# Twelve weight splits, each made one or two slots sooner, in a linear attention and rational feed-forward kernel

## Chip, cores and metric

The kernel runs on one core of one Trainium2 chip. The metric is the device time of one execution in microseconds (us); lower is better. A time stands as the median of several runs. One further execution was recorded by the hardware profiler, and all durations of single instructions come from that one.

## What is computed

Linear attention over 8 batches, 8 heads, 576 positions and 64 channels, with a normalisation of each head's output, and behind it a feed-forward layer whose activation is a quotient of two polynomials:

```python
kv  = einsum('bhsd,bhse->bhde', k, v)
out = einsum('bhsd,bhde->bhse', q, kv)
x   = out / sqrt(mean(out * out, axis=-1) + 1e-6) * g_norm   # then heads side by side: 4608 x 512
h   = x @ w_in                                               # 512 -> 2048
P   = a[0] + a[1] * h + a[2] * h**2 + a[3] * h**3
Q   = 1 + abs(b[0]) * abs(h) + abs(b[1]) * h**2
y   = (P / (Q + 1e-6)) @ w_out                               # 2048 -> 512
```

All inputs are float32. The kernel receives `w_in` and `w_out` as the 64-bit words that the host handed over (`I64` in the code) and makes float32 of them itself.

## The kernel before, in words

**Tiles and slots.** The 4608 tokens are cut into 9 tiles `t` of 512. In each tile the 2048 hidden channels are cut into 16 blocks `c` of 128. One pair (t, c) is a slot; the main loop (L657) runs over slots `i` = 16 t + c, 144 in all. In slot `i` the following is issued, engine by engine, in the order of the code (the scheduler is off, L605, so that each engine executes its instructions in just this order):

- ScalarE (ACT) and VectorE (DVE) turn the block `h` of slot `i` into the activation: `ew_a` (L472) begins with ACT's L477 on `h`, DVE's L479 makes `q`; `ew_d` (L506) splits the activation of slot `i - 1` into a rounded part `gh` (ACT, L513) and a rest `gl` (DVE, L514); `ew_b` and `ew_c` (L485, L493) finish with DVE's L503.
- TensorE (PE) does `gemm2` of slot `i - 2` (L517: 4 groups that add to `acc`), matmuls of the attention of the next tile, and `gemm1` of slot `i + 1` (L459: the `h` that ACT reads next). So PE works one to two slots ahead of and behind the elementwise engines. `h` has two buffers.

**Split weights.** In the first tile PE multiplies unsplit float32 operands (L463 for blocks below 8, L526). From the second tile on each product is done as three matmuls in a faster format: rest times high, high times low, high times high (L467 to L469 for `gemm1`, L530 to L532 for `gemm2`). For this each of the 16 weight units, ("wi", c) or ("wo", c), each holding two blocks, has to be split once into a high part and a low part. That takes three steps:

1. `split_w` (L219): ACT rounds the unit, 128 x 1024, into the high part (L231) at the end of the slot's `ew_b` work. It also notes the rest of the work in the list `lows`.
2. `low_by_transfer` (L236) in the *next* slot: POOL writes the negated high part into the low part's place (L237). A manual dependency holds this back until DVE has made `q` of that slot (L661).
3. POOL then issues a transfer of 512 KB which adds the float32 weight to that place (L238), so that weight minus high part is left. PE's L531 or L468 waits for this transfer to land.

The planner is a table written out by hand, `schedule` (L124): for each unit the slot of its fetch, of its conversion from 64-bit words, and, third, of its split; then the names of the memory cells of its raw words, of its float32 form and of its split form. The split form goes to cells that older units have left. A unit ("wi", c) is first used by `gemm1` of slot 16 + c, which PE does in slot 15 + c; a unit ("wo", c) by `gemm2` of slot 16 + c, which PE does in slot 18 + c. `at_slot(2, i)` (L674) picks the units to be split in slot `i`.

**What else lies around.** In the slots up to 15 the tile 0 work also contains the conversion of the last weights (ACT L195 and L188, DVE L207 and L215), the attention of tile 1 with its broadcast reads of the normalisation through DRAM (`att_rd`, `att_rb`, L409 to L423, on SP's queue), its use (`att_norm`, DVE L427) and the split of tile 1's `x` (ACT L290, DVE L294). In the second tile, slots 16 to 31, the attention of tile 2 takes slots 16 to 29, among them the reciprocal root (ACT L276 to L278) in slot 25, `att_norm` in slots 27 to 29 and the split of the new `x` in slot 30.

Of the kernel before, what the change touches and what calls it, by code (L numbers as in the profile page):

```python
# [23 lines left out]
def linear_attention_then_rational_ffn(  # L24
# [93 lines left out]
    def f32(t):  # L118
# [3 lines left out]


    schedule = {  # L124
# [16 lines left out]
    }  # L141
    units = list(schedule)

# [604 lines left out]
```

## Time and profile before

| | |
|---|---|
| median of 3 runs | 897.2 us (896.45 to 897.43) |
| the profiled execution's own time | 896.94 us |
| its span, first to last instruction | 895.2 us |
| granted clock of PE, mean | 0.997 of full |
| PE busy | 882.9 us, 99% |
| DVE busy | 768.4 us, 86% |
| ACT busy | 694.4 us, 78% |
| POOL busy | 77.9 us, 9% |

Times within the execution are in us from the start of the span. In a row of the timeline stand start, length, engine, line, operation, output<-inputs, and in brackets, if the engine sat idle before it, for how long and what ended that. A row of the waits gives who waited for whom, us in total, how often, and the longest. Matmuls overlap: their length is not what one costs; the distance between the starts of two neighbours is. A busy PE in the first table is therefore no proof that it waits for nothing.

### The profile page before, as it was taken

The numbers are of one execution on the slowest core, as the hardware profiler recorded it, in microseconds if no ns is written. First come the engines' busy times: TensorE is split into PE (matmuls) and PEld (weight loads), VectorE is DVE, ScalarE is ACT, GpSimd is POOL, SyncE is SP. The second block draws the span as 40 slices with busy tenths as digits, with TensorE's granted clock in tenths as the row PEclk, the third lists the DMA queues.
The fourth block names the chain that finished last, engine by engine and source line by source line (L and its number), as shares of the span: only waits on it lengthen the run. The fifth ranks groups of instructions, "written<-read, shape, count | busy, mean of one in ns | idle before, by whom it ended". The sixth has DMA issues, their size and how long they took to land.

```text
span 895.2 us, 11762 instructions
## 1 busy us (share of the span) xinstructions
PE 882.9 (99%) x4326; PEld 686.5 (77%) x4326; DVE 768.4 (86%) x1214; ACT 694.4 (78%) x1173; POOL 77.9 (9%) x85
## 2 busy tenths in 40 slices
PE   8999999998999999999999999999999999999998
PEld 5445567777787888878887888788878887888886
DVE  3888898878988898889978997899788988898887
ACT  5899979786887788777877787768767887777665
POOL 2053326413100000000000000000000000000000
PEclk9999999999999999999999999999999999999999
DMA  9997328534321203220320132012202020201001
GB/s 368 352 301 210 77 56 209 133 59 96 94 101 41 48 12 119 83 49 1 130 73 21 38 118 83 13 48 71 71 12 49 1 71 12 49 1 48 0 1 48
DMA packets 26810, 75.35 MB, mean 84 GB/s; under 512 B 2624, under 2 KB 2624, under 8 KB 26752
## 3 DMA queue, kind: packets, MB, share of 16 engines
q1 hardware_dynamic: 23328, 64.10, 20.8%
q0 software_dynamic: 2848, 9.44, 5.8%
q10 hardware_dynamic: 576, 1.05, 0.3%
q8 instruction: 34, 0.56, 0.3%
q14 instruction: 24, 0.20, 0.1%
HBM read 55.58 MB, written 9.57 MB: 73 GB/s over the span
## 4 chain that ended last, share of the span: by engine, by line
PE 78%; DVE 8%; ACT 7%; DMA 4%; issue 1%; POOL 1%; SPq 0%; DVEq 0%; POOLq 0%; ACTq 0%
PE h L467 12%; PE acc L531 12%; PE acc L532 12%; PE acc L530 12%; PE h L469 12%; PE h L468 12%; DMA wohl<-wow 2%; DVE q L479 2%; PE kvp L324 1%; DMA first<-in_first_dram 1%; DVE u L497 1%; PE ms L392 1%; DMA wol<-wow 1%; PE op L375 1%; PE op L376 1%
## 5 line engine op out<-in xcount | busy, mean ns | idle before, releaser
L477 ACT ACTIVATE d<-h 128x512 f32<-128x512 f32 x143 | 85.7, 599 | 154.9 <-PE h L469 152.1
L479 DVE SCALAR_TENSOR_TENSOR q<-d,b1abs,q 128x512 f32<-128x512 f32 x143 | 107.2, 750 | 96.6 <-ACT q L478 95.8
L467 PE MATMUL h<-x,wihl 128*128 128x512 f32 (+1 forms) x420 | 167.7, 399 | 0.0
L469 PE MATMUL h<-x,wihl 128*128 128x512 f32 (+1 forms) x420 | 162.8, 388 | 0.0
L468 PE MATMUL h<-x,wihl 128*128 128x512 f32 (+1 forms) x420 | 162.8, 388 | 0.0
L531 PE MATMUL acc<-wol,gh 128*128 128x512 f32 x316 | 123.7, 392 | 2.6 <-DMA wol<-wow 2.6
L530 PE MATMUL acc<-woh,gl 128*128 128x512 f32 x316 | 123.5, 391 | 0.8 <-DVE gl L514 0.8
L532 PE MATMUL acc<-woh,gh 128*128 128x512 f32 x316 | 123.4, 391 | 0.0
L490 ACT ACTIVATE d<-q,bias 128x512 f32<-128x512 f32 x143 | 105.7, 739 | 12.5 <-DVE q L479 11.1
L480 ACT ACTIVATE u<-h,na 128x512 f32<-128x512 f32 x143 | 112.6, 788 | 0.0
L491 ACT ACTIVATE d<-d,bias 128x512 f32<-128x512 f32 x143 | 103.6, 724 | 4.7
L497 DVE SCALAR_TENSOR_TENSOR u<-u,na,d 128x512 f32<-128x512 f32 x143 | 106.7, 746 | 0.0
L487 DVE SCALAR_TENSOR_TENSOR u<-u,na,h 128x512 f32<-128x512 f32 x143 | 106.1, 742 | 0.6
L495 DVE SCALAR_TENSOR_TENSOR q<-q,d 128x512 f32<-128x512 f32 x143 | 98.6, 690 | 0.2 <-ACT d L491 0.2
L481 DVE TENSOR_TENSOR u<-u,h 128x512 f32<-128x512 f32 x143 | 98.1, 686 | 0.4
L478 ACT ACTIVATE q<-h,abg 128x512 f32<-128x512 f32 x143 | 98.1, 686 | 0.0
L467 PEld LDWEIGHTS h<-x,wihl 128*128 128x128 f32 x420 | 78.9, 188 | 24.1 <-DVE gl L514 5.0
L468 PEld LDWEIGHTS h<-x,wihl 128*128 128x128 f32 x420 | 78.9, 188 | 16.7 <-issue 1.6
L469 PEld LDWEIGHTS h<-x,wihl 128*128 128x128 f32 x420 | 78.9, 188 | 16.5
L514 DVE TENSOR_TENSOR gl<-u,gh 128x512 fp32r<-128x512 f32 x127 | 91.1, 718 | 0.0
L503 DVE SCALAR_TENSOR_TENSOR u<-q,u 128x512 f32<-128x512 f32 x127 | 87.5, 689 | 2.4
L513 ACT CAST gh<-u 128x512 fp32r<-128x512 f32 x127 | 80.4, 633 | 3.5 <-DVE u L503 3.5
(153 smaller groups left out, 1443.0 us busy)
## 6 DMA issues: line engine op xcount, KB each, us to landing
kvm<-in_kv_dram SPq DMA_DIRECT2D x28, 640.0 KB
raw_wo<-in_w_out_dram SPq DMA_DIRECT2D x8, 1024.0 KB
qr<-in_qT_dram SPq DMA_DIRECT2D x32, 256.0 KB
out_dram<-ob SPq DMA_DIRECT2D x16, 512.0 KB
rb<-rd SPq DMA_DIRECT2D x28, 256.0 KB
raw_wi<-in_w_in_dram SPq DMA_DIRECT2D x6, 1024.0 KB
wihl<-wiw POOLq DMA_DIRECT2D x6, 512.0 KB, 4.7
first<-in_first_dram SPq DMA_DIRECT2D x4, 640.0 KB
```

The source lines that it names most:

```text
L467: PE.matmul(ph, wh, xl, start=(kc == 0), stop=False)
L468: PE.matmul(ph, wl, xh, start=False, stop=False)
L469: PE.matmul(ph, wh, xh, start=False, stop=(kc == NPAIR - 1))
L479: q_made = DVE.scalar_tensor_tensor(q, d, b1abs, q, ALU.mult, ALU.add)
L480: ACT.activation(u, ph, AF.Identity, bias=na[:, 2:3], scale=na[:, 3:4])
L487: DVE.scalar_tensor_tensor(u, u, na[:, 1:2], ph, ALU.add, ALU.mult)
L490: ACT.activation(d, q, AF.Ln, bias=bias[:, 2:3], scale=QSC)
L491: ACT.activation(d, d, AF.Exp, bias=bias[:, 3:4], scale=-1.0)
L497: DVE.scalar_tensor_tensor(u, u, na[:, 0:1], d, ALU.add, ALU.mult)
L530: PE.matmul(o, gl[:, ss], wh, start=(c == 0), stop=False)
L531: PE.matmul(o, gh[:, ss], wl, start=False, stop=False)
L532: PE.matmul(o, gh[:, ss], wh, start=False, stop=(c == NF - 1))
```

## The change

Only the third number, the slot of the split, changes, in twelve of the sixteen rows of `schedule`; code, cells, fetches and conversions stay.

```diff
-        ("wi", 0): (None, None, 12, "g0", "f0", "g3"),
+        ("wi", 0): (None, None, 11, "g0", "f0", "g3"),
...
-        ("wo", 10): (4, 9, 25, "g5", "f13", ("f5", "f4")),
+        ("wo", 10): (4, 9, 23, "g5", "f13", ("f5", "f4")),
```

| unit | wi 0 | wi 2 | wo 0 | wi 4 | wo 2 | wi 6 | wo 4 | wo 6 | wo 8 | wo 10 | wo 12 | wo 14 |
|---|---|---|---|---|---|---|---|---|---|---|---|---|
| split in slot, before | 12 | 14 | 15 | 16 | 17 | 18 | 19 | 21 | 23 | 25 | 27 | 29 |
| split in slot, now | 11 | 13 | 14 | 15 | 16 | 17 | 18 | 19 | 21 | 23 | 25 | 27 |

The negation on POOL and the transfer follow in the slot behind. As sets, the slots with a split lose 12 and 29 and gain 11 and 13; in the other ten a split stands as before, but that of a later unit.

The first place is ACT in slots 11 to 13. `wihl0` is the split form of ("wi", 0), `raw_wo12` the raw words of ("wo", 12), `d_0_12` the elementwise buffer of tile 0, block 12. Before:

```order
L490 ACTIVATE d_0_11_850<-q_0_11_851,bias_95 128x512
L491 ACTIVATE d_0_11_850<-d_0_11_850,bias_95 128x512
L195 ACTIVATE raw_wo12_632<-raw_wo12_632 128x1024
L188 ACTIVATE raw_wo12_632<-raw_wo12_632 128x1024
L477 ACTIVATE d_0_12_901<-h_0_12_882 128x512
L478 ACTIVATE q_0_12_902<-h_0_12_882,abg_118 128x512
L480 ACTIVATE u_0_12_903<-h_0_12_882,na_120 128x512
L490 ACTIVATE d_0_12_901<-q_0_12_902,bias_95 128x512
L491 ACTIVATE d_0_12_901<-d_0_12_901,bias_95 128x512
L231 CAST wihl0_917<-wiw0_279 128x1024
L477 ACTIVATE d_0_13_938<-h_0_13_919 128x512
```

The same place on ACT now:

```order
L490 ACTIVATE d_0_11_850<-q_0_11_851,bias_95 128x512
L491 ACTIVATE d_0_11_850<-d_0_11_850,bias_95 128x512
L231 CAST wihl0_868<-wiw0_279 128x1024
L195 ACTIVATE raw_wo12_632<-raw_wo12_632 128x1024
L188 ACTIVATE raw_wo12_632<-raw_wo12_632 128x1024
L477 ACTIVATE d_0_12_903<-h_0_12_884 128x512
L478 ACTIVATE q_0_12_904<-h_0_12_884,abg_118 128x512
L480 ACTIVATE u_0_12_905<-h_0_12_884,na_120 128x512
L490 ACTIVATE d_0_12_903<-q_0_12_904,bias_95 128x512
L491 ACTIVATE d_0_12_903<-d_0_12_903,bias_95 128x512
L477 ACTIVATE d_0_13_940<-h_0_13_921 128x512
```

The cast L231 of ("wi", 0) has moved in front of the conversion of ("wo", 12) in slot 11, and slot 12 has no cast left.

The second place is ACT in slot 23, tile 1, block 7, where the attention's `op` is read by L379 and L380. Before:

```order
L491 ACTIVATE d_1_7_1502<-d_1_7_1502,bias_95 128x512
L231 CAST woh8_1529<-wow8_702 128x1024
L379 ACTIVATE sq_2_3_1539<-op_2_3_1532 128x512
L380 COPY xf_2_3_1540<-op_2_3_1532 128x512
L477 ACTIVATE d_1_8_1559<-h_1_8_1543 128x512
```

And now:

```order
L491 ACTIVATE d_1_7_1507<-d_1_7_1507,bias_95 128x512
L231 CAST woh10_1534<-wow10_808 128x1024
L379 ACTIVATE sq_2_3_1544<-op_2_3_1537 128x512
L380 COPY xf_2_3_1545<-op_2_3_1537 128x512
L477 ACTIVATE d_1_8_1564<-h_1_8_1548 128x512
```

The slot keeps a cast of the same size, but it is that of ("wo", 10), which stood two slots later, in slot 25; ("wo", 8) is cast in slot 21. On POOL the sequence of negations and transfers is the same as before; each pair has moved against DVE's `q` that it waits for.

20 rows, old and new, of the table schedule are left out of this document.

## Prediction

> **What bounds the kernel now.** I read the page's busy times first, then the list of waits, then the windows, and last the timeline of PE around each wait.
>
> ```profile
> PE 882.9 (99%) x4326; PEld 686.5 (77%) x4326; DVE 768.4 (86%) x1214; ACT 694.4 (78%) x1173; POOL 77.9 (9%) x85
> ```
>
> ```profile
> ACT d L477 <- PE h L469: 152.1, 101, 5.7
> ```
>
> In 101 of 144 slots ACT, at the head of the elementwise work, waits for PE's `h`. PE is the bound; ACT and DVE have room. The windows (stretch, length, busy PE, PEld, DVE, ACT, POOL with counts, granted clock, DMA share, GB/s) say the same for the end of tile 1 and all that follows, and show one stretch at half clock:
>
> ```profile
> 17.00:208.00 191.00, 188.31 (x814) 119.72 (x814) 165.85 (x250) 167.05 (x263) 64.98 (x40) 1.00 0.61 181
> 208.00:211.04 3.04, 0.85 (x4) 0.38 (x2) 3.04 (x5) 2.92 (x5) 0.00 (x0) 1.00 0.80 159
> 211.04:214.45 3.41, 3.05 (x7) 2.48 (x8) 3.41 (x6) 1.57 (x3) 2.88 (x2) 0.50 0.01 5
> 214.45:891.00 676.55, 675.51 (x3381) 554.02 (x3379) 592.04 (x949) 515.62 (x887) 4.44 (x3) 1.00 0.16 49
> ```
>
> Behind 214.45 PE is idle for 1.0 us of 676. An edit that only moves work of ACT, POOL and the DMA can gain what PE loses by waiting before that, and nothing else. Four places in PE's timeline show loss that no later tile repeats. A slot without attention work sets the scale; seven of them in tile 2 took 38.08 us, so 5.44 us each and, with 24 matmuls, 0.227 us from one matmul to the next:
>
> ```profile
> 292.36:330.44 38.08, 38.08 (x170) 31.53 (x169) 35.81 (x56) 30.11 (x49) 0.00 (x0) 1.00 0.12 29
> ```
>
> **a.** `gemm2` of slot 16 reaches the low part of ("wo", 0):
>
> ```profile
> 146.77 0.39 PE L530 MATMUL acc<-wohl,gl 128*128 128x512 f32 x1
> 147.35 0.50 PE L531 MATMUL acc<-wohl,gh 128*128 128x512 f32 x1 [0.19 <-DMA wohl<-wow]
> ```
>
> The step is 0.58 us in place of 0.227: 0.35 us lost.
>
> **b.** `gemm2` of slot 20, the low part of ("wo", 4):
>
> ```profile
> 172.30 0.39 PE L530 MATMUL acc<-wohl,gl 128*128 128x512 f32 x1
> 173.84 0.47 PE L531 MATMUL acc<-wohl,gh 128*128 128x512 f32 x1 [1.15 <-DMA wohl<-wow]
> ```
>
> 1.54 - 0.23 = 1.31 us lost.
>
> **c.** `gemm2` of slot 26, the low part of ("wo", 10), and what follows it:
>
> ```profile
> 208.46 0.39 PE L530 MATMUL acc<-woh,gl 128*128 128x512 f32 x1
> 211.40 0.77 PE L531 MATMUL acc<-wol,gh 128*128 128x512 f32 x1 [2.55 <-DMA wol<-wow]
> ...
> 214.50 0.39 PE L532 MATMUL acc<-woh,gh 128*128 128x512 f32 x1
> ```
>
> From 208.46 to 214.50 PE goes eight steps, 1.82 us at full pace, in 6.04: 4.22 us lost. The wait itself is 2.94 - 0.23 = 2.71; the other 1.51 is the half clock of the window above, which begins inside the wait and ends at 214.45.
>
> **d.** `gemm2` of slot 30 waits for DVE, not for a transfer:
>
> ```profile
> 234.39 0.39 PE L469 MATMUL h<-x,wihl 128*128 128x512 f32 x1
> 235.59 0.50 PE L530 MATMUL acc<-woh,gl 128*128 128x512 f32 x1 [0.81 <-DVE gl L514]
> ```
>
> The rest `gl` of slot 30 is made late, in slot 31. 1.20 - 0.23 = 0.97 us lost.
>
> **The change part by part.** First the transfers. In the chain of waits, each transfer of b and c stands with its start and its time to landing:
>
> ```profile
> 164.40 9.30 DMA wohl<-wow
> ```
>
> ```profile
> 204.29 6.97 DMA wol<-wow
> ```
>
> ("wo", 4) moves from slot 19 to 18, so its transfer leaves where that of ("wi", 6) left; ("wo", 10) moves from slot 25 to 23, where ("wo", 8) left:
>
> ```profile
> 158.06 0.89 POOL L238 DMA_DIRECT2D wil<-wiw  x1 [0.30 <-POOL wil L237]
> ...
> 190.80 0.90 POOL L238 DMA_DIRECT2D wol<-wow  x1 [0.30 <-POOL wol L237]
> ```
>
> Even with the slowest landing seen, 9.30, they are down at 167.4 and 200.1, and PE wants them at 172.5 and 208.7: 5 and 8 us of room. ("wo", 0) gains a slot, which is 5 us and more against a loss of 0.35. The others wait for nothing today and come sooner still. So a, b and c go whole: 0.35 + 1.31 + 4.22 = 5.88 us. The half clock goes with its wait, since no other stretch at half clock is in the trace after 17 us.
>
> The number of casts, negations and transfers is unchanged. Ten slots keep a cast. Slots 11 and 13 gain one, 12 and 29 lose one; negations leave 13 and 30 and come to 12 and 14. The cost is in these slots.
>
> *Slots 11 to 14.* A cast sets ACT back by 0.94 us from start to start:
>
> ```profile
> 126.47 1.03 ACT L231 CAST wihl<-wiw 128x1024 fp32r<-128x1024 f32 x1
> 127.41 1.14 ACT L290 CAST x<-xf 128x512 fp32r<-128x512 f32 x2
> ```
>
> In slot 11 ACT runs without a gap into slot 12, and DVE's first operation there follows it at once:
>
> ```profile
> 110.41 0.75 DVE L479 SCALAR_TENSOR_TENSOR q<-d,b1abs,q 128x512 f32<-128x512 f32 x1
> ```
>
> So from slot 12 on DVE is 0.94 us late. Slot 12, now without cast, doesn't give this back, because from there to slot 14 DVE is the later of the two. The second added cast, in slot 13, is hidden by just this: ACT waits 1.51 us for DVE in slot 14,
>
> ```profile
> 125.09 0.72 ACT L490 ACTIVATE d<-q,bias 128x512 f32<-128x512 f32 x1 [1.51 <-DVE q L479]
> ```
>
> and 0.94 fits into 1.51. If that cover were gone it would cost another 0.94. What decides is whether PE notices. The tightest place is `gemm2` of slot 14:
>
> ```profile
> 130.04 0.69 DVE L503 SCALAR_TENSOR_TENSOR g<-q,u 128x512 f32<-128x512 f32 x1
> ```
>
> ```profile
> 132.03 2.31 PE L526 MATMUL acc<-wow,g 128*128 128x512 f32 x5
> ```
>
> Ready at 130.73, used at 132.03: 1.30 us of room, 0.36 after the delay. The next tight place is slot 17's `gl`, made in slot 18:
>
> ```profile
> 149.95 1.15 DVE L514 TENSOR_TENSOR gl<-u,gh 128x512 fp32r<-128x512 f32 x1
> ```
>
> ```profile
> 152.69 0.39 PE L530 MATMUL acc<-wohl,gl 128*128 128x512 f32 x1
> ```
>
> 1.59 us of room; minus 0.94, minus the 0.35 that PE is sooner by a, leaves 0.30. By slot 21 the waits of ACT for PE have swallowed the delay. I put slots 11 to 20 at nothing, with 1.0 us as the upper end (both rooms just missed, and both casts on the path: 1.88 - 1.30 = 0.6, and 0.4 at slot 17).
>
> *Negations.* Beside a negation DVE's L514 takes 1.17 us (149.95 above: 1.15) in place of 0.69. In tile 0 there is no L514. What stands there beside a negation is L215, once without one (slot 12) and once with one (slot 13, POOL busy from 117.31):
>
> ```profile
> 112.47 0.68 DVE L215 CUSTOM_DVE_ANT_0 wow<-raw_wo,wow 128x1024 uint16<-128x1024 uint16 x1
> ...
> 118.50 0.68 DVE L215 CUSTOM_DVE_ANT_0 wow<-raw_wo,wow 128x1024 uint16<-128x1024 uint16 x1
> ```
>
> ```profile
> 117.31 2.76 POOL L237 TENSOR_SCALAR wihl<-wihl 128x1024 fp32r<-128x1024 f32 x1 [7.55 <-DVE q L479]
> ```
>
> The same 0.68: the new negations in slots 12 and 14 cost DVE nothing. The Trainium skill's page "SBUF — State Buffer", section "Who interferes with whom", says that a VectorE instruction with two SBUF inputs and a GpSimd instruction that reads SBUF exclude each other, and that the later one blocks fully. The trace shows 0.48 us on L514 and none on L215.
>
> *Slots 28 to 31.* This is where d lies, and where part of c's gain could be lost: while PE waited in c, DVE caught up.
>
> ```profile
> 219.58 0.75 DVE L479 SCALAR_TENSOR_TENSOR q<-d,b1abs,q 128x512 f32<-128x512 f32 x1 [3.53 <-ACT q L478]
> ```
>
> ```profile
> 225.34 0.75 DVE L479 SCALAR_TENSOR_TENSOR q<-d,b1abs,q 128x512 f32<-128x512 f32 x1
> ```
>
> ```profile
> 229.90 0.69 DVE L294 TENSOR_TENSOR x<-xf,x 128x512 fp32r<-128x512 f32 x1 [0.88 <-ACT x L290]
> ```
>
> ```profile
> 233.58 0.75 DVE L479 SCALAR_TENSOR_TENSOR q<-d,b1abs,q 128x512 f32<-128x512 f32 x1
> 234.25 0.68 DVE L481 TENSOR_TENSOR u<-u,h 128x512 f32<-128x512 f32 x1
> 234.84 0.69 DVE L514 TENSOR_TENSOR gl<-u,gh 128x512 fp32r<-128x512 f32 x1
> ```
>
> On the clock of before: DVE was done with slot 28 at 219.58 - 3.53 = 216.05. Slot 29 takes it 225.34 - 219.58 = 5.76, slot 30 8.24, less 0.48 for the negation that leaves and less the 0.88 wait: 6.88. It begins slot 31 at 228.69, and `gl` is done 1.95 later, at 230.64. PE without its wait begins `gemm2` of slot 30 four slots of 5.44 after 208.46, at 230.22. It waits 0.42 us. Of d, 0.97 - 0.42 = 0.55 us is gained. (In slots 25 to 28 each cast and negation is replaced by one of the same size, so the rooms there stay.)
>
> **Sum.** 5.88 + 0.55 = 6.43 us off the profiled execution's 896.94 us gives 890.5. That execution lay 0.26 us under the median, so for a median I say **890.8**.
>
> **The rivals.**
>
> *DVE becomes the bound.* Slots 11 to 14 or 28 to 31 are tighter than I count them: up to 1.0 us at the first, and all of d back (0.55) at the second, and with PE sooner by 4 us up to 0.6 more there. For it: rooms of 0.36 and 0.30 are small against sums of a dozen rows. Against: tile 2 has the same elementwise work and no wait of PE. Time: 891.3 to 893.0.
>
> *Blocking in full.* Were L215 and what follows held until the negation ends, slots 12 and 14 would cost DVE 1.5 us each (`q` takes 0.75 and the negation behind it 2.76, 3.5 in all; L215 starts 112.47 - 110.41 = 2.06 after `q`). 0.94 + 2.9 - 1.30 = 2.5 us: 893.3. The two equal rows of L215 speak against it. This is what the rule of "SBUF — State Buffer" in the Trainium skill, named above, would make of it.
>
> *The half clock stays.* If the stretch at half clock were not owed to the wait, it would cost its 1.51 us anyway: 892.3. The Trainium skill, "TensorE: Matmul & The Clock Gate", Part 1, says that PE drops to half clock after at least one idle window of about 3.4 us; by that rule a wait of 2.55 us would be too short to cause it. The trace speaks against the rule: the only half clock begins inside the longest wait.
>
> *No effect.* The landing is set by something else than the issue, for instance by other traffic on the 16 DMA engines, and PE waits as before: 897.2. That two landings differ as 6.97 and 9.30 do is for it; the room of 5 and 8 us speaks against.
>
> *Slower.* The transfer of ("wi", 0) now leaves a slot sooner, just ahead of SP's second set of broadcast reads in slot 12, on which `att_norm` in slot 13 and with it `x` of tile 1 depend. If it holds them back, DVE stands still in slot 13. DVE has 0.36 us of room there; each us more is a us of PE. The gain is eaten at 0.4 + 6.4 = 6.8 us of delay, and the run is slower by 0.2% (1.8 us) from 8.6 us on. The two landings above differ by 2.33 us, so a delay of nearly four times that is needed. Time then: 899.
>
> **How the numbers follow.** A measurement of this kernel can tell about 0.2%, 1.8 us, from no change. Chances: forecast 0.64 (890.0 to 891.5: all of d or none of it), DVE the bound 0.22, blocking 0.04, half clock 0.04, no effect 0.03, slower 0.03. Faster by more than 0.2% are the first four, 0.94; the same 0.03; slower 0.03. The range takes the forecast with the 0.5 us by which runs of before lie off their middle, and the first rival: 889.5 to 893.0. It leaves out about 0.1.
>
> **What would show it.** Right: no wait of PE L531 for `wohl` or `wol`; no stretch at half clock; PE's wait for `gl` near slot 30 at 0.5 us or less; DVE about 0.9 us later in slots 12 to 16, without a wait of PE for `g`. Wrong: PE waits for DVE at `gemm2` of slots 14 or 17, a long L427 in slot 13, L215 longer than 0.7 in slots 12 and 14, or a new transfer that PE stands before.

## The result, and the profile after

| | before | after |
|---|---|---|
| median | 896.83 us (4 runs, 895.89 to 897.43) | 890.72 us (4 runs, 890.69 to 890.77) |
| profiled execution | 896.94 us, span 895.2 us | 890.70 us, span 888.9 us |

The ratio after to before is 0.9933, 95% interval 0.9916 to 0.995: faster by 0.7%. The forecast was 890.8 us in a range of 889.5 to 893.0.

The page's busy share of PE is 99% as before. Of the 6.3 us by which the span is shorter, 4.1 were idle time of PE (12.3 before, 8.2 now); the other 2.2 stood inside its busy time, as longer matmuls at half clock and as waits that the modelled length of the matmul in front covers:

```profile
PE 880.7 (99%) x4326; PEld 685.7 (77%) x4326; DVE 767.6 (86%) x1214; ACT 694.6 (78%) x1173; POOL 77.9 (9%) x85
```

In the windows the clock now stays whole to the last microseconds (column PEclk, the third from the right):

```profile
17.00:240.00 223.00, 220.86 (x995) 146.78 (x994) 198.52 (x303) 194.40 (x309) 72.30 (x44) 1.00 0.58 169
240.00:880.00 640.00, 640.00 (x3193) 525.60 (x3192) 561.45 (x895) 490.46 (x843) 0.00 (x0) 1.00 0.15 48
```

PE's timeline shows matmuls 0.23 us apart at the places a, b and c, where there were waits; its last two rows are place d:

```profile
146.72 0.39 PE L530 MATMUL acc<-wohl,gl 128*128 128x512 f32 x1
146.95 0.39 PE L531 MATMUL acc<-wohl,gh 128*128 128x512 f32 x1
...
171.77 0.39 PE L530 MATMUL acc<-wohl,gl 128*128 128x512 f32 x1
172.00 0.39 PE L531 MATMUL acc<-wohl,gh 128*128 128x512 f32 x1
...
206.51 0.39 PE L530 MATMUL acc<-woh,gl 128*128 128x512 f32 x1
206.74 0.39 PE L531 MATMUL acc<-wol,gh 128*128 128x512 f32 x1
...
228.16 0.39 PE L469 MATMUL h<-x,wihl 128*128 128x512 f32 x1
229.37 0.50 PE L530 MATMUL acc<-woh,gl 128*128 128x512 f32 x1 [0.82 <-DVE gl L514]
```

At d it is 1.21 us from one row to the next, as before (1.20), so nothing was gained there. At slot 14 DVE has become later, but not late:

```profile
130.84 0.69 DVE L503 SCALAR_TENSOR_TENSOR g<-q,u 128x512 f32<-128x512 f32 x1
...
150.76 1.15 DVE L514 TENSOR_TENSOR gl<-u,gh 128x512 fp32r<-128x512 f32 x1
```

```profile
131.98 1.02 PE L526 MATMUL acc<-wow,g 128*128 128x512 f32 x2
...
152.16 0.39 PE L530 MATMUL acc<-wohl,gl 128*128 128x512 f32 x1
```

`g` of slot 14 is ready at 131.53, 0.45 us before PE takes it (1.30 before the change), `gl` of slot 17 at 151.91, 0.25 us before (1.59).

### The profile page after: what moved, and what is told of

It is laid out like the page before. It is cut to its first block, busy times and chain, and to the rows that moved or that the text cites. A ratio compares the mean times of both kernels' runs of the same rounds, so it can differ in the third digit from the quotient of the medians.

```text
span 888.9 us, 11762 instructions
## 1 busy us (share of the span) xinstructions
PE 880.7 (99%) x4326; PEld 685.7 (77%) x4326; DVE 767.6 (86%) x1214; ACT 694.6 (78%) x1173; POOL 77.9 (9%) x85
## 4 chain that ended last, share of the span: by engine, by line
PE 97%; DMA 1%; DVE 1%; ACT 0%; SPq 0%; issue 0%; ACTq 0%
PE h L467 14%; PE h L469 14%; PE h L468 14%; PE acc L530 13%; PE acc L531 13%; PE acc L532 13%; PE acc L526 6%; PE h L463 3%; PE kvp L324 2%; DMA first<-in_first_dram 1%; PE ms L392 1%; PE op L375 1%; PE op L376 1%; PE op L374 1%; PE op L370 0%; DVE x L294 0%
## 5 line engine op out<-in xcount | busy, mean ns | idle before, releaser
L495 DVE SCALAR_TENSOR_TENSOR q<-q,d 128x512 f32<-128x512 f32 x143 | 98.6, 690 | 0.2 <-ACT d L491 0.2
L514 DVE TENSOR_TENSOR gl<-u,gh 128x512 fp32r<-128x512 f32 x127 | 90.6, 714 | 0.0
L503 DVE SCALAR_TENSOR_TENSOR u<-q,u 128x512 f32<-128x512 f32 x127 | 87.5, 689 | 2.4
```

## Experiments

The theory is that the gain is made of waits for transfers, each worth its own length and, for the long one, the half clock behind it; that a cast added in slot 11 costs nothing as long as DVE's room at slots 14 and 17 holds; and that d is no matter of the splits. The rivals are in the expectations. All twelve were timed beside the kernel before, whose medians in the four groups were 895.50, 896.61, 896.29 and 896.73 us; single executions of it lie between 894.64 and 898.87 but for one at 900.82.

These 56 executions of the kernel before are of two kinds, by the granted clock that is on record for each. A stretch of 3.41 us at half clock takes 0.002 off the mean over 895 us. In 35 of them the mean is 0.998 or less, and their median is 896.73 us; in 21 it is 0.999 or 1.000, and their median is 895.09. So the kernel before had its stretch at half clock in about five executions of eight, at a price of 1.6 us, and its median over a few executions depends on how many of each kind are among them. The changed kernel has 0.999 or 1.000 in all of its executions.

The medians of the experiments:

| kernel | what it is | median us | ratio to before (95%) |
|---|---|---|---|
| c_alone | before, only ("wo", 10) sooner | 892.17 | 0.9955 (0.9941 to 0.997) |
| ab_alone | before, five splits up to ("wo", 4) sooner | 894.94 | 0.9984 (0.9974 to 0.9994) |
| last_two_alone | before, only ("wo", 12), ("wo", 14) sooner | 896.45 | 1.0 (0.9991 to 1.0009) |
| wo10_later | after, ("wo", 10) in slot 26 | 898.71 | 1.0029 (1.0018 to 1.0039) |
| both_in_11 | after, ("wi", 2) also in slot 11 | 894.85 | 0.9978 (0.9967 to 0.9989) |
| three_in_11 | after, ("wi", 2), ("wi", 4) also in slot 11 | 895.88 | 0.9997 (0.9987 to 1.0006) |
| first_at_12 | after, ("wi", 0) in slot 12 | 890.63 | 0.9937 (0.9922 to 0.9952) |
| x_cells | after, other cells for `x` | 889.92 | 0.9929 (0.9913 to 0.9946) |
| cast_twice | after, cast in slot 11 doubled | 891.70 | 0.9946 (0.9932 to 0.9961) |
| cast_thrice | after, cast in slot 11 tripled | 892.83 | 0.9959 (0.9944 to 0.9974) |
| x_cells_12 | x_cells and first_at_12 | 889.87 | 0.9926 (0.9909 to 0.9943) |
| both_in_12 | after, ("wi", 0), ("wi", 2) in slot 12 | 891.47 | 0.9943 (0.9921 to 0.9965) |

### One wait at a time

**c_alone**

```diff
-        ("wo", 10): (4, 9, 25, "g5", "f13", ("f5", "f4")),
+        ("wo", 10): (4, 9, 24, "g5", "f13", ("f5", "f4")),
```

> The kernel before with one number changed: ("wo", 10) split in slot 24 in place of 25. Theory (the gain is the waits for late transfers, each wait by itself): its wait of 2.71 us and the half clock behind it, 1.5 us, go, the waits for ("wo", 0) and ("wo", 4) stay: 4.2 us less, 892.6 us, and no stretch at half clock in the middle of the span. Rival (DVE needs that pause, and takes the time back in slots 28 to 31): 1 to 2 us less, 895 to 896. Rival (the half clock is not owed to the wait): 2.7 us less, 894.1.

892.17 us, 0.4 less than expected. The window around place c has no half clock:

```profile
200.00:220.00 20.00, 20.00 (x90) 16.56 (x89) 19.70 (x31) 15.42 (x24) 3.66 (x2) 1.00 0.44 91
```

One number out of twelve brings most of the whole: 890.72 + 1.45 = 892.17, and 1.45 is about what a and b are left to cost. Beside the executions of the kernel before in the same group it is 2.92 us less than those at a granted clock of 0.999 or 1.000 (median 895.09) and 4.63 less than the others (896.80): the wait alone, and the wait with the half clock. In the list of waits of this kernel, between 100 and 240 us, PE waits for `wohl` and for `gl`, no more for `wol`:

```profile
PE acc L531 <- DMA wohl<-wow: 1.0, 2, 0.8
PE acc L530 <- DVE gl L514: 0.8, 1, 0.8
```

The wait for ("wo", 4) is 0.8 us here in place of 1.15, which is the 0.4 that the expectation missed. DVE does not take the pause back: PE's wait for it, the second row, is as long as ever.

**ab_alone**

```diff
-        ("wo", 0): (None, None, 15, "g2", "f2", "g7"),
-        ("wi", 4): (-1, 0, 16, "g3", "f3", ("f6", "f8")),
-        ("wi", 6): (-1, 1, 18, "g4", "f4", ("f10", "f12")),
-        ("wo", 2): (-1, 1, 17, "g5", "f5", "g1"),
+        ("wo", 0): (None, None, 13, "g2", "f2", "g7"),
+        ("wi", 4): (-1, 0, 15, "g3", "f3", ("f6", "f8")),
+        ("wi", 6): (-1, 1, 17, "g4", "f4", ("f10", "f12")),
+        ("wo", 2): (-1, 1, 16, "g5", "f5", "g1"),
...
-        ("wo", 4): (0, 3, 19, "g7", "f7", "e"),
+        ("wo", 4): (0, 3, 18, "g7", "f7", "e"),
```

> The kernel before with five splits moved: ("wo", 0) 15 to 13, ("wi", 4) 16 to 15, ("wo", 2) 17 to 16, ("wi", 6) 18 to 17, ("wo", 4) 19 to 18. Theory: the waits for ("wo", 0) and ("wo", 4) go, 0.46 and 1.39 us with the slow first step behind each, the wait for ("wo", 10) stays as it is, since its transfer and PE both come 1.85 us sooner: 895.0 us. If the half clock hangs on how the wait lies to fixed stretches of 3.41 us, counted from the start of the record, it may go as well, because the wait now lies across two of them: then 893.5. Rival (the early part gains nothing, because ACT's extra cast in slot 13 costs as much): 896.8.

894.94 us in the median; the profiled execution took 894.85 (before: 896.94, so 2.1 less) and still waits for ("wo", 10), as its list of waits for the same stretch says:

```profile
PE acc L531 <- DMA wol<-wow: 2.5, 1, 2.5
PE acc L530 <- DVE gl L514: 0.8, 1, 0.8
```

The waits for `wohl` are gone and that for `wol` is as before, with a stretch at half clock of 3.41 us behind it. Of its ten executions four lie between 893.22 and 893.80, all at a granted clock of 1.000, and six between 894.85 and 895.58, at 0.997 or 0.998: by that, four were without the half clock. Each kind beside its like in the same group, the gain is 1.72 us (893.37 against 895.09) and 1.60 us (895.20 against 896.80), where the two waits had been put at 1.85; the ratio of 0.9984 mixes the two kinds. That four were without half clock need not come from the moved wait, since the kernel before has such executions too.

**last_two_alone**

```diff
-        ("wo", 12): (6, 11, 27, "g7", "f14", ("f7", "f9")),
-        ("wo", 14): (8, 13, 29, "g1", "f15", ("f11", "f13")),
+        ("wo", 12): (6, 11, 26, "g7", "f14", ("f7", "f9")),
+        ("wo", 14): (8, 13, 28, "g1", "f15", ("f11", "f13")),
```

> The kernel before with ("wo", 12) split in slot 26 in place of 27 and ("wo", 14) in 28 in place of 29. Theory: nothing waits for these two, so 896.8 us, and PE waits for gl in slot 31 as before, 0.97 us. Rival (taking the cast out of slot 29 and the negation out of slot 30 relieves DVE, as the prediction counted): 0.5 us less or more, 896.3 or lower, with a shorter wait for gl.

896.45 us, ratio 1.0. (The median lies above that of its group, 895.50, because seven of ten executions here have a granted clock of 0.998 or less, against ten of 23 of the kernel before.) PE's wait for `gl` is unchanged:

```profile
PE acc L530 <- DVE gl L514: 0.8, 1, 0.8
```

Taking the cast out of slot 29 and the negation out of slot 30 gives nothing, against the step d of the prediction.

**wo10_later**

```diff
-        ("wo", 10): (4, 9, 23, "g5", "f13", ("f5", "f4")),
+        ("wo", 10): (4, 9, 26, "g5", "f13", ("f5", "f4")),
```

> The changed kernel with one number moved the other way: ("wo", 10) split in slot 26, one slot later than in the kernel before. Theory: its transfer leaves at about 207.3 us and lands 4.5 to 7 us later, PE wants it at 206.7: a wait of 5 to 7.6 us and a half clock that costs 1.7 us or more behind it: 897.3 to 900.2 us. Rival (the landing is set by other traffic, not by the slot of the split): 890.7 to 893.

898.71 us, 8.0 more than after. The chain of waits before the place, PE's rows and the windows:

```profile
204.23 2.77 POOL wol L237
207.29 4.96 DMA wol<-wow
212.39 0.76 PE acc L531
```

```profile
206.47 0.39 PE L530 MATMUL acc<-woh,gl 128*128 128x512 f32 x1
212.39 0.76 PE L531 MATMUL acc<-wol,gh 128*128 128x512 f32 x1 [5.53 <-DMA wol<-wow]
```

```profile
205.00:209.15 4.15, 1.86 (x9) 1.20 (x7) 4.15 (x7) 3.56 (x6) 2.89 (x2) 1.00 1.06 213
209.15:215.97 6.82, 3.58 (x9) 2.84 (x10) 5.68 (x8) 1.94 (x3) 3.26 (x2) 0.50 0.33 64
```

The transfer leaves at 207.29, as expected, lands after 4.96 us, and PE waits 5.9 - 0.2 = 5.7 us for it. The half clock lasts 6.82 us, twice as long as before; 3.24 of them fall into the wait, the other 3.58 behind it. The landing follows the split.

### The added cast in slot 11

**both_in_11** and **three_in_11**

```diff
-        ("wi", 2): (None, None, 13, "g1", "f1", "g5"),
+        ("wi", 2): (None, None, 11, "g1", "f1", "g5"),
```

three_in_11 has ("wi", 4) in slot 11 as well, in place of 15.

> The changed kernel with ("wi", 2) split in slot 11 as well, in place of 13: two casts on ACT there. Theory (ACT's delay in slot 11 goes on to DVE, and PE notices what exceeds its room): DVE is another 0.94 us late. In the changed kernel g of slot 14 is ready 0.44 us and gl of slot 17 0.25 us before PE takes them, so PE now waits 0.5 us at the first and some 0.2 us at the second: 891.3 to 891.6. Rival (the delay is taken up by the slots without a cast, 12 and 13): 890.7.

> The changed kernel with ("wi", 2) and ("wi", 4) split in slot 11 as well, in place of 13 and 15: three casts on ACT there. Theory: DVE is 1.88 us later than in the changed kernel, PE waits 1.44 us for g of slot 14 and up to 0.2 us for gl of slot 17: 892.2 to 892.5, so 0.9 us for the third cast, where the first cost nothing. Rival (the delay is taken up): 890.7.

894.85 and 895.88 us: 4.1 and 5.2 over after, 3 us more than expected. From the second to the third cast it is 1.03 us, as the theory has it; the level is not. DVE's timeline of both_in_11 in slots 12 and 13:

```profile
116.26 2.33 DVE L503 SCALAR_TENSOR_TENSOR g<-q,u 128x512 f32<-128x512 f32 x1
...
126.00 0.75 DVE L427 SCALAR_TENSOR_TENSOR xf<-xf,ghalf,rb_qh 128x512 f32<-128x512 f32 x1 [1.36 <-DMA rb_qh<-rd]
```

and POOL's:

```profile
113.00 2.76 POOL L237 TENSOR_SCALAR wihl<-wihl 128x1024 fp32r<-128x1024 f32 x1 [3.38 <-DVE q L479]
116.06 0.89 POOL L238 DMA_DIRECT2D wihl<-wiw  x1 [0.30 <-POOL wihl L237]
116.67 3.12 POOL L237 TENSOR_SCALAR wihl<-wihl 128x1024 fp32r<-128x1024 f32 x1
```

Two things besides ACT's 0.94 us have come up. L503, usually 0.69 us, takes 2.33 beside the second negation. And the second transfer now leaves at 120.09, in the midst of the broadcast reads; these go out late themselves, because their cells come free only when DVE is done with the first L427 (119.26):

```profile
119.29 0.44 SPq L418 DMA_DIRECT2D rb_qh<-rd  x1
...
120.44 0.60 SPq L418 DMA_DIRECT2D rb_qh<-rd  x1
```

`att_norm` waits 1.36 us for them. In cast_thrice (below), where the reads go out nearly as late, at 118.82, but beside no second transfer, it does not wait. Together 0.94 + 1.64 + 1.36 = 3.9 us of delay, and PE waits at the next place where DVE and ACT hold it up:

```profile
131.40 0.47 PE L467 MATMUL h<-x,wihl 128*128 128x512 f32 x1 [2.09 <-ACT d L491]
```

followed by half clock again (from 131.93 for 3.41 us). That is not what costs here: five of the ten executions have a granted clock of 0.999 or 1.000 and took 894.58 to 895.14 us, the other five have 0.998 and took 894.75 to 895.10. By that, PE loses what exceeds its room of DVE's 3.9 us either way, slowed or waiting. Both are mechanisms that the prediction had put among the rivals, for one split in slot 12's negation; there they did not occur, with two they do.

**cast_twice** and **cast_thrice** take the second negation and transfer away again and leave only ACT's delay (the cast is simply done over). Lines from 232 on count one higher here.

```diff
-        ACT.copy(wh, w)
+        for _ in range(2 if u == ("wi", 0) else 1):
+            ACT.copy(wh, w)
```

cast_thrice has 3 in place of 2.

> The changed kernel with the cast of ("wi", 0) in slot 11 done twice over; negations and transfers as they are. Theory (with no second negation in slot 12, only ACT's delay is left, and PE notices what exceeds its room): DVE 0.94 us later, against rooms of 0.44 us for g of slot 14 and 0.25 us for gl of slot 17: PE waits 0.5 us and about 0.2 us, no half clock: 891.3 to 891.6. Rival (the 4 us that the second split in slot 11 cost are ACT's delay after all): 894 or more.

> The same with three casts of ("wi", 0) in slot 11. Theory: DVE 1.88 us later than in the changed kernel, PE waits 1.44 us for g of slot 14 and 0.2 us for gl of slot 17: 892.2 to 892.6, or 1.5 us more where the wait brings a half clock. Rival as for the twofold cast: 895 or more.

891.70 and 892.83 us: 0.98 and 2.11 over after, without half clock, and 0.1 and 0.2 over the upper ends of the expectations. The first added cast (in the changed kernel) cost nothing, the second 0.98, the third 1.13. PE's row of cast_twice at slot 14 shows what stands there now, and further on slot 17 the same:

```profile
132.68 1.55 PE L527 MATMUL acc<-wow,g 128*128 128x512 f32 x3 [0.34 <-DVE g L504]
```

So the room was real and of about the size read from the rows. DVE's `q` of slot 12 starts at 112.30 and 113.32 in place of 111.20, 1.10 and 2.12 us later rather than 0.94 and 1.88; less the smaller room of 0.25 that is 0.85 and 1.87. The rest is slow steps: a matmul behind a wait comes late even to the next one, 153.41 - 153.07 = 0.34 us in place of 0.23 at slot 17.

```profile
153.07 0.50 PE L531 MATMUL acc<-wohl,gl 128*128 128x512 f32 x1
153.41 0.40 PE L532 MATMUL acc<-wohl,gh 128*128 128x512 f32 x1
```

**first_at_12**

```diff
-        ("wi", 0): (None, None, 11, "g0", "f0", "g3"),
+        ("wi", 0): (None, None, 12, "g0", "f0", "g3"),
```

> The changed kernel with ("wi", 0) back in slot 12. Theory: the cast in slot 12 lies beside ACT's wait for DVE, DVE is not late any more, and PE had not noticed the delay: 890.7, with the rooms at slots 14 and 17 back to 1.3 and about 1.2 us. Rival (the cast in slot 11 costs time already): 890 or less.

890.63 us, 0.09 under after. `g` of slot 14 is ready at 130.47 and taken at 131.80: the room is back to 1.33 us. Moving the first split brought nothing and cost next to nothing.

**both_in_12** puts the two back-to-back negations where ACT is not late and the broadcast reads are over.

```diff
-        ("wi", 0): (None, None, 11, "g0", "f0", "g3"),
-        ("wi", 2): (None, None, 13, "g1", "f1", "g5"),
+        ("wi", 0): (None, None, 12, "g0", "f0", "g3"),
+        ("wi", 2): (None, None, 12, "g1", "f1", "g5"),
```

> The changed kernel with ("wi", 0) and ("wi", 2) both split in slot 12, so that both negations follow each other in slot 13 and no cast stands where ACT is late. Theory (with two splits in slot 11, DVE's L503 took 2.33 us because of the second negation and its neighbour, and the broadcast reads came late because the transfers were ahead of them): L503 of slot 13 takes about 2.3 us again, the reads are through before the transfers start, so PE notices 1.65 us less DVE's room of 1.3: 0.35 us, 891.0 to 891.2. Rival (L503 was held by the traffic of transfers and reads, not by the negation): 890.6 to 890.7.

891.47 us, somewhat more than expected (0.75 over after). In the profile PE is 0.39 us later than in after from slot 14 on (132.79 against 132.41), as expected, and 0.58 from slot 17 on (152.97 against 152.39), which the expectation had left out. DVE's and POOL's rows:

```profile
120.39 2.34 DVE L503 SCALAR_TENSOR_TENSOR g<-q,u 128x512 f32<-128x512 f32 x1
122.66 0.74 DVE L427 SCALAR_TENSOR_TENSOR xf<-xf,ghalf,rb_qh 128x512 f32<-128x512 f32 x1
```

```profile
120.81 3.12 POOL L237 TENSOR_SCALAR wihl<-wihl 128x1024 fp32r<-128x1024 f32 x1
```

No read is waited for, and L503 takes 2.34 us again. It is the second negation that holds it, and not the issue of the first transfer, which stands beside it too: in the kernel before, where L503 of this slot stands beside such an issue alone, it takes 0.69 us.

```profile
120.37 0.90 POOL L238 DMA_DIRECT2D wihl<-wiw  x1 [0.30 <-POOL wihl L237]
```

```profile
120.57 0.69 DVE L503 SCALAR_TENSOR_TENSOR g<-q,u 128x512 f32<-128x512 f32 x1
```

### Place d

**x_cells**

```diff
-            xs[t, p // 2] = xpool.tile([P, 2, 2, TW], F32R, tag=("xA", "xB")[p // 2 ^ (t == 1)], name=f"x_{t}_{p}")
+            xs[t, p // 2] = xpool.tile([P, 2, 2, TW], F32R, tag=("xA", "xB")[p // 2 ^ (t >= 1)], name=f"x_{t}_{p}")
```

> The changed kernel with one comparison changed, t == 1 to t >= 1, in the choice of the cells for the split x: the new x of tile 2 then begins with the cell whose last reader is the first half of gemm1 of slot 31, not its second half. Theory (PE's wait for gl of slot 30 comes from DVE standing 0.76 us until ACT may cast x, which waits for the whole of that gemm1): the 0.76 go, the wait of 0.98 us shrinks to 0.2: 889.9. Rival (DVE is simply full there, and the wait is its load): 890.7.

889.92 us, 0.80 under after. In the changed kernel ACT waits 1.04 us for PE before it may cast the new `x`, and DVE after it; these are its rows for the two engines:

```profile
223.03 2.18 ACT L290 CAST x<-xf 128x512 fp32r<-128x512 f32 x4 [1.04 <-PE h L469]
```

```profile
223.69 0.69 DVE L294 TENSOR_TENSOR x<-xf,x 128x512 fp32r<-128x512 f32 x1 [0.76 <-ACT x L290]
```

and in x_cells, ACT and PE at the same place:

```profile
221.77 2.32 ACT L290 CAST x<-xf 128x512 fp32r<-128x512 f32 x4
```

```profile
227.96 0.39 PE L469 MATMUL h<-x,wihl 128*128 128x512 f32 x1
228.40 0.50 PE L530 MATMUL acc<-woh,gl 128*128 128x512 f32 x1
```

The step is 0.44 us in place of 1.21. In tile 1 the cells of `x` are swapped, so that the first new half goes where the half lies which `gemm1` of slot 31 reads last; the wait runs from PE over ACT and DVE back to PE, and no split can shorten it.

**x_cells_12** joins this with first_at_12.

> The changed kernel with the other choice of cells for x (t >= 1) and ("wi", 0) back in slot 12. Theory: the first takes 0.8 us, the second nothing but gives DVE its room back: 889.8 to 889.9, the lowest of all.

889.87 us: as x_cells, and with it the lowest here. Its distance to x_cells is within the spread of either.

## Why the prediction was right, point by point

**a, b, c.** Right, in mechanism and size. The prediction took 5.88 us for them, 0.35, 1.31 and 4.22. The starts of the same matmul in the two profiles are 0.05 us apart ahead of a (146.77 and 146.72), 0.53 ahead of b (172.30 and 171.77), 1.95 ahead of c (208.46 and 206.51) and 6.23 ahead of d (234.39 and 228.16): 0.48, 1.42 and 4.28, together 6.18. The three transfers now leave at 135.42, 158.95 and 188.84; the slowest landing in this trace is 8.7 us, and PE wants them at 146.95, 172.00 and 206.74. c_alone and ab_alone remove the waits separately, wo10_later lengthens one, and the transfer's time of leaving decides each time. What the prediction left out is the slow first step behind a wait, 0.1 us at a and at b.

**The half clock goes with its wait.** Right: no execution profiled without the wait shows it before the last microseconds, and no execution of the changed kernel has a granted clock under 0.999. The rival in which it stays falls. But the term of 1.51 us was taken for a fixed part of the wait, and it is not: every profiled execution with a wait of over 2 us has the half clock, yet by the granted clock 21 of 56 executions of the kernel before were without it. The three behind the prediction's median, and the profiled one, were by their times all of the other kind, which was luck. That the 21 had the waits all the same is read from their times alone: 4.37 us lie between their median and the changed kernel, as much as a, b and the wait of c make without the half clock (0.35 + 1.31 + 2.71).

**Slots 11 to 20 cost nothing.** Right. DVE was to be 0.94 us late; its `q` of slot 12 starts 0.79 later (111.20 against 110.41). The prediction gave PE 0.36 and 0.30 us of room; 0.45 and 0.25 were measured, and cast_twice shows that PE pays as soon as that is used up. The rival "DVE becomes the bound" was one cast away.

**Negations cost DVE nothing in tile 0.** Right for this change, but the reason given, two equal rows of L215, was too narrow: it matters which part of the negation an operation meets. The nine L514 beside a negation in the trace of before began 0.35 to 0.54 us into it and took 1.23 to 1.04 us, so that each ended 1.57 to 1.59 us after the negation's start. An L514 takes 0.69 us by itself, so each of them got going about 0.9 us into the negation, however early it had begun. The negation beside the prediction's row of 149.95:

```profile
149.53 2.78 POOL L237 TENSOR_SCALAR wohl<-wohl 128x1024 fp32r<-128x1024 f32 x1 [3.28 <-DVE q L479]
```

L215 starts 1.2 us into its negation (118.50 against 117.31 before, 113.26 against 112.06 now), behind that part, and so it was not held. L503, 4 us after `q`, was never beside a negation in the trace of before. both_in_11 and both_in_12 put it there, and it took 1.65 us more; like L514 it ended 1.2 us ahead of the negation's end. The rule of the Trainium skill, "SBUF — State Buffer", "Who interferes with whom", by which a VectorE instruction with two SBUF inputs is blocked by a GpSimd one that reads SBUF, fits these rows in part. L503 ended at 122.73 and the negation by its row only at 123.93, and L495, with two such inputs as well, stands beside the later part of a negation (119.11) and takes 0.69 us.

**Broadcast reads held back.** The prediction's slower rival named this, at a chance of 0.03. With one transfer ahead it did not show; with two the reads came 1.36 us too late.

**d.** Here the prediction failed. The step was: slot 30 takes DVE "8.24, less 0.48 for the negation that leaves and less the 0.88 wait: 6.88". It took 7.64 (219.73 to 227.37). The negation's 0.48 went (L514 in slot 30 is at 0.68), but the wait remained, 0.76, since ACT's cast of `x` hangs on PE's `gemm1` of slot 31: it comes sooner just as far as PE comes sooner, and so cannot be taken off. x_cells shows what ends it. 0.55 us was forecast for d, and none came: PE loses 1.21 - 0.23 = 0.98 us there, where 0.42 had been forecast. (The prediction's own sentence that nothing behind 214.45 can be gained left no place for d, which lies at 235.)

**The sum.** Forecast were 6.43 us off the profiled execution, and 6.24 came (896.94 to 890.70): 0.30 more than forecast for a, b and c, of which the slow steps are the likeliest part, 0.55 less for d, and 0.06 that belong to no place. Two errors of opposite sign partly cancel. That the median came nearer still, 890.72 against 890.8, is luck: the forecast added the 0.26 us by which the profiled execution of before lay under its median, and that of after lies only 0.02 under its own.

## What to carry to other kernels

Where one engine is the bound, look at what it does between two neighbouring instructions, not at its busy time: three pairs of rows held all of a gain of 0.7% here, a fourth looked like them and held none of it, and one number in twelve was worth two thirds of it. A table of due times needs room on both sides: read for each moved step how long its result now lies ready, and how long the engine that does it has before someone waits, and do not count a wait as removed before you have found out what ends it. Steps that share an engine pair (here DVE and POOL) are to be kept one per slot, since two in a row reach operations that one never touched. And look at the granted clock of every execution before comparing medians: one kernel can have two kinds of execution.

## What the runs showed of the hardware

- In the profiles, waits of PE of 2.09 us (both_in_11), 2.55 (before) and 5.53 (wo10_later) each brought a stretch at half clock of 3.41 us or twice that; waits of 1.15 us (before, place b) and less brought none. The Trainium skill, "TensorE: Matmul & The Clock Gate", Part 1, asks for an idle window of about 3.4 us; less than that was enough here.
- Such a wait does not always bring it: 35 of 56 executions of the kernel before have a granted clock of 0.998 or less, 21 have 0.999 or 1.000. In all six profiles with an early stretch at half clock it begins a whole number of times 3.413 us after the first entry of the trace's clock record: 60 times in before, ab_alone, last_two_alone and wo10_later, 37 times in both_in_11 and three_in_11. That fits a clock that is set anew every 3.413 us by what PE did since the last time; that this decides which executions are spared is not shown.
- A negation on POOL (2.76 us) holds a DVE operation that reads two tiles in SBUF only in its first 0.9 us: L514 took 1.04 to 1.23 us there in place of 0.69, while L215 and L495, later beside the same negations, took 0.68 and 0.69 as ever. Beside the second of two negations in a row L503 took 2.33 us in place of 0.69; by its row it had begun 0.4 us ahead of that negation, and why it was held all the same is open.
- A matmul that ends a wait is followed after 0.31 to 0.34 us, not 0.23 (0.34 at a, 0.31 at b of the kernel before).
